# One load of modulation weights split in two, with the scale half in front of the shift half

## The chip, the core and the metric

The kernel runs on one core of a Trainium2 chip. The metric is the device time of one execution in microseconds (us). The core has a matrix engine (TensorE, PE in the profile), whose weight loads are listed apart (PEld), a vector engine (VectorE, DVE), a scalar engine (ScalarE, ACT), GpSimd (POOL) and SyncE (SP), which here does nothing but issue transfers (DMAs). Sixteen DMA engines carry the transfers of all queues.

## The reference

The input is one sequence of 2048 tokens with 640 features in bfloat16. A conditioning vector gives six modulation vectors; the block is an adaptive layer norm ahead of a spectral filter, and another ahead of a gated feed-forward layer.

```
mod = (silu(c) @ w_mod)                 # w_mod: [640, 6*640]
sa, ca, ga, sb, cb, gb = mod split in six
h = layernorm(x) * (1 + ca) + sa
x = x + ga * irfft2(rfft2(h) * W)       # W: [2048, 321] complex
h = layernorm(x) * (1 + cb) + sb
x = x + gb * ((silu(h @ w_gate) * (h @ w_up)) @ w_down)   # 1728 hidden
```

The change concerns sb and cb, the shift and the scale of the second layer norm. Each is the product of a 640-vector with a 640x640 block of w_mod, 800 KB in bfloat16.

## The kernel before

The whole computation is one straight program. The order of the instructions on each engine and in each queue is the order in which the Python code emits them; no scheduler reorders anything. An engine waits in place for the semaphores of what its next instruction needs, and what stands behind it on that engine waits too.

The stages, in order of time:

1. Forward transform (to about 35 us). For each of 16 token tiles TensorE transposes the tile (`t1`), transforms it over the features (`dfwd`) and adds it into a transform over the tokens (`s1`). The result lies in `A_sb`.
2. Spectral filter (to about 63 us). The feature frequencies are worked off in 21 groups of mostly four (`groups`, `NG` = 21). For group g, `stage_a` transforms on TensorE (L567) and multiplies with the filter on VectorE (`prod`, L592); `stage_b` (L599) sums on TensorE; `stage_c` (L620) transforms back; `evac` and `rot` (L637, L648) copy out. The loop runs `stage_a` two groups ahead of `stage_b`.
3. Inverse transform over the token tiles (63 to 82 us), t = 0 to 15: `s1em` and `s1er` (L669, L678) with the table `Htab`, then L1184 and L1187 with the table `RI`, and VectorE adds the residual into `x1` (L1189). `RI` is first multiplied by ga on VectorE (L724, L728). Within this loop the second layer norm of the first two tiles is made: statistics (L761 on ScalarE, L765 to L771), normalization (L775), a transpose by DMA in SP's queue (L789), then scale and shift of the transposed columns, four on GpSimd (L797) and the fifth on ScalarE (L803). TensorE first needs them in `gu13` (L1001).
4. Feed-forward layer in four chunks of 2, 4, 4 and 6 token tiles (82 us to the end): gate and up products (L1013, L1043), down products (L891, L914), residual and store (L883, L884). Some of the weights are combined into tables first; GpSimd issues accumulating loads for that (`gu_dma`, L823).

The modulation weights: `wm_r` holds the four blocks ga, sb, cb, gb of w_mod as `wm_r[:, :, j, :]`, j = 0 to 3, on 128 partitions with 5 rows each. Block 0 is loaded early (L279). Blocks 1 and 2 are loaded by one DMA of 1600 KB (L527), block 3 by one of 800 KB (L528). Both stand in SP's queue behind the four DMA transposes of `A_sb` (`t2_dma`, L519), which wait for the end of stage 1, and ahead of the tables `Htab` and `RI` (L529, L530), the loads of w_down (L734 to L738) and those of the gate and up weights (L741, L742, `load_gu` at L746).

The columns of cb and sb are computed on TensorE in the gaps of the filter stage, as 5 column blocks of 5 matmuls each (`mod_col`, L580), inside `stage_a` behind the group's first matmul. Group NG-4 = 17 takes column blocks 0 and 1 of block j = 2 (scale), group 18 the same of j = 1 (shift), group 19 the rest of the scale, group 20 the rest of the shift:

```
for i, l in enumerate(ls):
    ...
    if i == 0:
        for c5 in {NG - 4: (0, 1), NG - 3: (0, 1), NG - 2: (2, 3, 4), NG - 1: (2, 3, 4)}.get(g, ()):
            mod_col(psum[:, 2 + 2 * (g % 2), 192 + c5:193 + c5], wm_r[:, :, 1 + g % 2], c5)
```

The results are copied at L704 and L705. Block 3 follows behind the last `stage_c` (L719).

Of the kernel before, what the change touches and what calls it, by code (L numbers as in the profile page):

```python
# [155 lines left out]
def adaln_block_kernel(ctx, tc, A_x, A_w_r, A_w_i, B_x, B_w_gate, B_w_up, B_w_down, c, w_mod, out):  # L156
    nc = tc.nc
# [55 lines left out]
    wm_r = rM.cut(12800, [NC5, 4, D])  # L213
# [64 lines left out]
    wm_m = wm_v[:, :, 2 * D:6 * D].rearrange("p k (i d) -> p k i d", i=4)  # L278
# [233 lines left out]
    if True:  # L512
        B2of = {}

        def t2_dma(bi):
            l0 = (1, 16, 32, 64)[bi]
            n = 15 if bi == 0 else 16
            B2b = rL.cut(4096 * bi, [16, 128]) if bi < 3 else rM.cut(6144, [16, 128])
            nc.sync.dma_start_transpose(B2b[:, :n, :], A_sb[:, l0:l0 + n, :, :, :].rearrange("p l t c r -> p l (t c r)"))  # L519
            for i in range(n):  # L520
                B2of[l0 + i] = (B2b, i, l0, n)
# [2 lines left out]
        t2_dma(1)  # L524
        t2_dma(2)
        t2_dma(3)
        nc.sync.dma_start(wm_r[:, :, 1:3, :], wm_m[:, :, 1:3, :])  # L527
        nc.sync.dma_start(wm_r[:, :, 3, :], wm_m[:, :, 3, :])  # L528
        nc.sync.dma_start(Htab[:], H_dram)  # L529
        nc.sync.dma_start(RI[:], RI_dram)  # L530
        Wd_sb = rA.cut(0, [NFC, D])
# [743 lines left out]
@with_exitstack  # L1275
def kernel(
    ctx: ExitStack,
    tc: tile.TileContext,
    A_x: bass.AP,
    A_w_r: bass.AP,  # L1280
    A_w_i: bass.AP,
    B_x: bass.AP,
    B_w_gate: bass.AP,
    B_w_up: bass.AP,
    B_w_down: bass.AP,
    c: bass.AP,
    w_mod: bass.AP,
    out: bass.AP,
):
    with tc.manual_schedule():  # L1290
        adaln_block_kernel(tc, A_x, A_w_r, A_w_i, B_x, B_w_gate, B_w_up, B_w_down, c, w_mod, out)
# [30 lines left out]
```

## Time and profile before

| | |
|---|---|
| time, median of 3 runs | 249.32 us (249.18 to 249.86) |
| the profiled execution's own time | 249.31 us |
| its span, first to last instruction | 247.5 us |
| granted TensorE clock | 1.000 |
| TensorE busy | 241.5 us |
| VectorE / ScalarE / GpSimd busy | 207.7 / 167.8 / 78.1 us |
| the 1600 KB load (L527): issue, time to landing | 48.06 us, 7.32 us |
| the 800 KB load behind it (L528): issue, time to landing | 48.7 us, 10.2 us |

In the profile's lines, L527 is line 527 of the kernel. Times are counted from the start of the span. A timeline's row has start, length, engine, line, operation, output <- input, and the count of instructions merged into the row; in brackets stands the idle time before it and what ended it. Matmuls are pipelined and their ends are modelled, so the starts of successive matmuls say more than the lengths. The names are those of the memory regions: `rM` holds the modulation weights and later `x1`, `rW` the filter and later the gate and up weights, `rA` first `A_sb` and later the w_down weights, `rH` the tables `Htab` and `RI`. In the transfer windows, q1 is the queue that SP issues into and q0 that of GpSimd.

### The profile page before, as it was taken

How to read it: one execution, taken by the hardware profiler on the slowest of the kernel's cores; microseconds unless marked ns; L12 is line 12 of the kernel's file. 1: busy time of each engine (PE TensorE's matmuls, PEld its weight loads, DVE VectorE, ACT ScalarE, POOL GpSimd, SP SyncE). 2: the span in 40 equal slices, each digit the busy share in tenths (PEclk: the TensorE clock that was granted, in tenths of full speed). 3: DMA queues.
4: the chain of work that ended last, by engine and by line, in shares of the span. 5: the costliest groups of instructions: out<-in, count | busy, mean ns of one | idle time of the engine just before them, and what ended most of it. 6: DMA issues, size and time to landing. Idle time of an engine off the chain costs nothing.

```text
span 247.5 us, 6173 instructions
## 1 busy us (share of the span) xinstructions
PE 241.5 (98%) x2327; PEld 189.7 (77%) x2327; DVE 207.7 (84%) x516; ACT 167.8 (68%) x327; POOL 78.1 (32%) x128
## 2 busy tenths in 40 slices
PE   8999999999999999999999999999999999999994
PEld 3778877989999888688887778887765666656773
DVE  3799699988898998789989977788998787789864
ACT  3778757996989698489774488866246777773220
POOL 8577765993243605002004400000432000004400
PEclk9999999999999999999999999999999999999999
DMA  7999999999999999600005110200411000000111
GB/s 220 396 361 315 307 391 177 179 337 392 295 348 317 298 280 187 139 15 3 0 3 106 53 55 3 57 0 19 93 49 53 3 0 1 4 0 0 53 56 53
DMA packets 45760, 34.74 MB, mean 140 GB/s; under 512 B 21732, under 2 KB 42659, under 8 KB 45347
## 3 DMA queue, kind: packets, MB, share of 16 engines
q1 hardware_dynamic: 43936, 30.00, 42.7%
q0 software_dynamic: 1504, 4.28, 7.4%
q8 instruction: 18, 0.29, 0.5%
q10 hardware_dynamic: 290, 0.08, 0.1%
q14 instruction: 12, 0.09, 0.1%
HBM read 27.05 MB, written 4.72 MB: 128 GB/s over the span
## 4 chain that ended last, share of the span: by engine, by line
PE 89%; DVE 4%; DMA 3%; issue 1%; ACT 0%; POOL 0%; DVEq 0%; SPq 0%; ACTq 0%; POOLq 0%
PE psum L1043 36%; PE psum L914 19%; PE psum L1013 6%; PE psum L891 3%; DMA rM<-in_w_mod_dram 3%; PE psum L669 3%; PE psum L599 2%; PE psum L296 2%; PE psum L1184 2%; PE psum L1187 2%; PE psum L1001 2%; PE psum L567 2%; DVE rE L382 2%; PE psum L318 1%; PE psum L315 1%; PE psum L393 1%
## 5 line engine op out<-in xcount | busy, mean ns | idle before, releaser
L1043 PEld LDWEIGHTS <-rW 128*128 128x128 bf16 (+1 forms) x429 | 42.0, 98 | 12.6
L1043 PE MATMUL psum<-rW 128*128 128x256 bf16 (+1 forms) x247 | 42.2, 287 | 0.0
L940 POOL TENSOR_TENSOR rM<-rM,rL 128x320 f32<-128x320 f32 x6 | 5.4, 906 | 96.6 <-ACT rL L939 96.6
L914 PEld LDWEIGHTS <-rE 128*128 128x128 f16 (+1 forms) x196 | 19.0, 97 | 7.8
L914 PE MATMUL psum<-rE 128*128 128x320 f16 (+1 forms) x147 | 22.9, 299 | 0.0
L592 DVE TENSOR_TENSOR rM<-psum,rW 128x384 bf16<-128x384 f32 (+2 forms) x42 | 20.2, 543 | 2.7 <-PE psum L567 1.2
L1074 ACT COPY rH<-psum 128x384 f32<-128x384 f32 (+2 forms) x27 | 14.0, 517 | 7.4 <-PE psum L1043 6.0
L1081 ACT COPY rX<-psum 128x384 f32<-128x384 f32 (+2 forms) x27 | 14.0, 520 | 7.2 <-PE psum L1043 7.0
L1043 PEld LDWEIGHTS <-rE 128*128 128x128 f16 x156 | 15.3, 98 | 4.7
L1078 DVE TENSOR_TENSOR rH<-psum,rM 128x512 bf16<-128x512 f32 (+1 forms) x24 | 15.0, 624 | 4.4 <-PE psum L1043 2.2
L1097 ACT ACTIVATE rL<-psum 128x384 bf16<-128x384 f32 (+2 forms) x27 | 14.4, 533 | 5.3 <-PE psum L1043 3.4
L1082 DVE TENSOR_TENSOR rX<-psum,rX 128x384 f32<-128x384 f32 (+2 forms) x27 | 16.3, 604 | 1.6 <-ACT rX L1081 1.4
L1068 ACT COPY rM<-psum 128x384 f32<-128x384 f32 (+2 forms) x27 | 13.9, 516 | 4.2 <-PE psum L1043 4.2
L382 DVE SCALAR_TENSOR_TENSOR rE<-rE,mv,psum 128x648 bf16<-128x648 f32 (+1 forms) x17 | 14.2, 840 | 2.1 <-PE psum L318 1.7
L1043 PE MATMUL psum<-rW,rE 128*128 128x256 bf16 (+1 forms) x78 | 15.6, 290 | 0.0
L1043 PE MATMUL psum<-rE,rY 128*128 128x256 f16 (+1 forms) x78 | 15.6, 290 | 0.0
L338 ACT COPY rE<-psum 128x640 bf16<-128x640 bf16 x16 | 11.1, 693 | 6.1 <-PE psum L336 5.1
L1098 ACT ACTIVATE rL<-rX 128x384 bf16<-128x384 f32 (+2 forms) x27 | 15.1, 559 | 0.0
L1013 PE MATMUL psum<-rW 128*128 128x256 bf16 x130 | 14.5, 272 | 0.0
L602 ACT CAST rY<-psum 128x512 bf16<-128x512 f32 (+2 forms) x21 | 11.8, 574 | 3.9 <-PE psum L599 3.6
L1189 DVE SCALAR_TENSOR_TENSOR rM<-psum,rX 128x640 f32<-128x640 f32 x16 | 13.0, 820 | 1.7 <-PE psum L1187 1.6
L883 DVE TENSOR_TENSOR rA<-psum,rM 128x320 bf16<-128x320 f32 (+1 forms) x27 | 12.1, 472 | 2.4 <-PE psum L891 2.3
(223 smaller groups left out, 666.5 us busy)
## 6 DMA issues: line engine op xcount, KB each, us to landing
out_dram<-rA SPq DMA_DIRECT2D x31, 80.0 KB, 1.6
rM<-in_w_mod_dram SPq DMA_DIRECT2D x3, 800.0 KB, 10.2
rX<-in_A_x_dram SPq DMA_DIRECT2D x3, 640.0 KB, 7.4
rA<-in_B_w_down_dram SPq DMA_DIRECT2D x2, 960.0 KB, 14.4
rY<-in_B_w_gate_dram POOLq DMA_DIRECT2D x2, 832.0 KB, 7.9
rM<-in_w_mod_dram SPq DMA_DIRECT2D x1, 1600.0 KB, 7.3
rW<-in_B_w_gate_dram SPq DMA_DIRECT2D x2, 640.0 KB, 7.1
rW<-in_B_w_up_dram SPq DMA_DIRECT2D x2, 640.0 KB, 7.1
```

The lines of the kernel that those rows point to most:

```text
L382: nc.vector.scalar_tensor_tensor(Zv[:, h], Cv[:, h], mv[:, t, 0:1], zps[:, h], ALU.mult, ALU.subtract)
L592: nc.vector.tensor_tensor(PP[:, :, hl], xv[:, :, hl], in1, ALU.mult)
L914: nc.tensor.matmul(o, lhsT=lhs[rows(k), k], rhs=rhs[rows(k), k], start=start and k == ks[0], stop=stop and k == ks[-1], skip_group_check=True)
L1013: nc.tensor.matmul(gu[u], lhsT=Wgu[:, u, c5, ff * 128:(ff + 1) * 128], rhs=h2T[:, :, c5, :], start=(c5 == 0), stop=(c5 == NC5 - 1))
L1043: nc.tensor.matmul(o[:, f], lhsT=w, rhs=b, start=(start and f == 0 and i == 0), stop=(stop and f == len(groups[g]) - 1 and i == len(ops) - ...
L1068: nc.scalar.copy(c0, X)
L1074: nc.scalar.copy(c2, X)
L1078: nc.vector.tensor_tensor(c11, Z, c0, ALU.add)
L1081: nc.scalar.copy(c3, X)
L1082: nc.vector.tensor_tensor(c22, Y, c3, ALU.add)
L1097: nc.scalar.activation(g21, X, ACT.Silu, scale=-1.0)
L1098: nc.scalar.activation(g22, c22, ACT.Silu, scale=-1.0)
```

## The change

The one DMA of blocks 1 and 2 becomes two of one block each. The scale block (j = 2) is issued first, then the shift block (j = 1), then block 3 as before, which now is the third turn of the same loop.

```
-        nc.sync.dma_start(wm_r[:, :, 1:3, :], wm_m[:, :, 1:3, :])
-        nc.sync.dma_start(wm_r[:, :, 3, :], wm_m[:, :, 3, :])
+        for j in (2, 1, 3):
+            nc.sync.dma_start(wm_r[:, :, j, :], wm_m[:, :, j, :])
```

The bytes are the same. In w_mod the two blocks lie side by side, so that a row of the one DMA is 2560 contiguous bytes, and a row of each of the two is 1280. SP's queue has one entry more; the order of the others in it, and the order on every other engine, stay. TensorE's wait ahead of the scale columns is now for the scale block alone, and a wait for the shift block stands ahead of the first matmul of the shift columns in group 18. In the kernel after, all three loads carry the line L528, and all other lines keep their numbers.

## The prediction

> **What bounds the kernel now.** I read the page first, then the chain of waits, then timelines and transfer windows around the edited load, and last the first place behind it where another engine joins TensorE.
>
> The page says that TensorE is the bound: 98% of the span, so a gain must come out of its 6 us of gaps.
>
> ```profile
> span 247.5 us, 6173 instructions
> PE 241.5 (98%) x2327; PEld 189.7 (77%) x2327; DVE 207.7 (84%) x516; ACT 167.8 (68%) x327; POOL 78.1 (32%) x128
> ```
>
> The chain of waits between 44 and 68 us (start, length, what) has one transfer in it, the edited one.
>
> ```profile
> 47.88 0.13 SPq L519
> 48.02 0.04 issue
> 48.06 7.32 DMA rM<-in_w_mod_dram
> 55.38 0.05 issue
> 55.43 0.40 PE psum L580 x10
> ```
>
> It leaves SP's queue at 48.06, right behind the last transpose (L519), lands at 55.38, and TensorE starts the scale columns (L580) 0.05 later. How long TensorE stood is in its timeline (start, length, instructions, idle before):
>
> ```profile
> 54.59 0.25 PE L567 MATMUL psum<-Ktab,rM 128*128 128x192 bf16 x1
> 55.43 0.40 PE L580 MATMUL psum<-sc_col,rM 128*128 128x1 bf16 x10 [0.59 <-DMA rM<-in_w_mod_dram]
> ...
> 56.38 0.25 PE L567 MATMUL psum<-Ktab,rM 128*128 128x192 bf16 x1
> 56.46 0.39 PE L580 MATMUL psum<-sc_col,rM 128*128 128x1 bf16 x10
> ```
>
> The second pair, which waited for nothing, starts 0.08 us apart; the first pair 0.84 apart. The stall is worth 0.76 us of issue time (the 0.59 counts from the modelled end of the matmul). The line at 56.46 is the first use of the shift columns, 1.03 us behind the scale columns, and no wait stands before it: both halves are in one transfer today.
>
> **The change, part by part.** The sum is made against the profiled execution's 249.31 us (span 247.5 and 1.8 around it), 0.01 below the median of 249.32.
>
> *Removed:* the wait for 1600 KB before the scale columns. The 800 KB of the scale go first. Transfers start slowly here (42 packets of 2560 B between 48.9 and 50.4 us), then run at full rate:
>
> ```profile
> DMA packets 157, 0.40 MB, mean 402 GB/s; under 512 B 0, under 2 KB 0, under 8 KB 157
> ```
>
> That is 52.5 to 53.5 us. From 50.4 on, 0.82 MB take 2.0 us at this rate; with the tail of the slowest engine (about 1 us: the load would be through at 54.4 by rate and landed at 55.38) the scale lands by 53.5, over 1 us before TensorE can use it at 54.59 + 0.08 = 54.67. **Gain there: 0.76 us**, and PE's place at the shift columns moves to 56.46 - 0.76 = 55.70.
>
> *Added:* a second wait, PE's for the shift half. The same bytes have passed by then, in rows of 1280 B in place of 2560. The neighbour L528, of just this shape, moves between 55 and 56 us as follows:
>
> ```profile
> DMA packets 289, 0.37 MB, mean 370 GB/s; under 512 B 0, under 2 KB 289, under 8 KB 289
> ```
>
> One engine is busy with something else in that window, so 370 against 402 GB/s is the dear bound: 1.64 MB take 0.35 us longer. The cheap bound is 0: from 52 to 54 us (2560 B alone) 403 GB/s flowed, from 54 to 56 (nearly all 1280 B) 388. I take 0.2. The shift half then lands at 55.38 + 0.2 = 55.58, 0.12 ahead of its use; at the dear bound it comes at 55.73 and costs 0.1. **Term: 0.** Behind that wait stand the rest of the group's transforms and all of TensorE, and DVE's products (L592), which wait for them.
>
> *SP's queue:* one more issue of about 0.52 us (L528's row) ahead of the last gate columns, Htab, RI and the W_down loads. Nothing is fetched later for that: the transfer engines are full from 50.4 on and those wait behind bytes, not behind the issue. What they do inherit is the 0.2. Their covers, after PE's move: column 3 at 58.9 + 0.2 for a use at 62.18 - 0.76; Htab at 61.46 + 0.2 for 63.03 - 0.76 = 62.27; RI at 62.23 + 0.2 for DVE's L724 at 63.32 - 0.76 = 62.56. RI is the tightest, 0.13; beyond that it costs one to one, up to 0.15 at the dear bound. **Term: 0.**
>
> [...]
>
> *Given back further on.* From 55.4 to 80 us TensorE has hardly a gap, DVE and ACT wait for it, and all move 0.76 forward. The next thing that does not hang on TensorE is the transposed, normalized input of the first token chunk: SP's L789 issues the transpose at 72.19, it lands at 78.09, GpSimd scales four of five columns (L797), TensorE uses them at 80.79.
>
> ```profile
> 70.20 0.84 POOL L823 DMA_DIRECT2D rY<-in_B_w_gate_dram  x1
> 78.22 2.50 POOL L797 TENSOR_SCALAR rW<-rW,one_p_cb,modcols 128x256 bf16<-128x256 bf16 x4 [7.17 <-DMA rW<-rL]
> ```
>
> ```profile
> 80.79 0.71 PE L1001 MATMUL psum<-rW,Wp 128*128 128x256 bf16 x5
> ```
>
> L1001's matmuls stand 0.11 apart, so the fourth, which needs GpSimd's last column (80.72, plus 0.05), runs at 81.11. **The slack is 0.34 us, less than the 0.76 that TensorE brings**; what decides is whether the landing at 78.09 moves too. It is a matter of bytes: the third gate/up load (L746, issued 68.35) and GpSimd's 832 KB load (L823) are ahead of the transpose. Between 74.5 and 75 us L823's queue has the engines for itself:
>
> ```profile
> DMA packets 60, 0.20 MB, mean 399 GB/s; under 512 B 0, under 2 KB 0, under 8 KB 60
> ## 3 DMA queue, kind: packets, MB, share of 16 engines
> q0 software_dynamic: 60, 0.20, 114.0%
> ```
>
> L823 follows GpSimd's chain from DVE's first L1189 and so also starts 0.76 earlier, into the third L746 load. At 73.0 - 0.76 = 72.24 that load has 0.2 MB (200 packets after 73.0) + 0.76 us x 0.354 MB/us + the inherited 0.07 = 0.54 MB left; with L823's 0.85 MB that is 1.39 MB at 0.39 MB/us, 3.6 us, ending at 75.8. The same sum for today's order gives 75.7 where the trace ends at 76.3, so I allow 75.8 to 76.3 and take 76.1 for the transpose's first packet (today 75.1). Its data need 1.3 us (492 packets in the half microsecond from 77.0, some 1280 in all) if its list is ready, 2.3 as today (75.1 to 77.4) if it starts slowly, and 0.65 to land. That is 78.05 to 79.05; I take 78.25, near the quick end, as it will have been queued for a microsecond. GpSimd is then through 78.25 - 78.09 = 0.16 later than today, TensorE's L1001 comes 0.34 - 0.16 = 0.18 earlier, and behind it TensorE runs without a gap to the end.
>
> **Sum:** -0.76 at L580, +0.58 at L1001: -0.18, **249.1 us**. Its own range: landing 77.9 to 78.5, 248.8 to 249.4.
>
> **The rivals.**
>
> *All of it is kept* (0.20): the transpose lands 0.42 earlier or more, because it has its list early and slips in between the two loads. An unloaded transpose of this size (L789 at 155.60) takes 3.8 us, from 71.43 that is 75.2. Against it: one queue, in order, with the third L746 load ahead. 249.31 - 0.76 = 248.55.
>
> *Slower, at the same join* (0.16): the transpose starts at 76.3, has today's slow 2.3 us and lands at 79.25. GpSimd ends 1.16 later, TensorE loses 1.16 - 0.34 = 0.82: 250.1. The deciding point is a landing after 78.43; 79.2 makes 0.3%. For it: the transpose's packets were slow even with the engines half idle.
>
> *Slower, at the shift half* (0.04): the second half does not flow behind the first but starts anew, in the 2.3 us from issue (48.06) to full rate (50.4). It lands at 57.7, against 56.46 today: +1.2, 250.5. Against it: between 54 and 55 us packets of both sizes flow without a pause. [...]
>
> *It does not do what it says* (0.12): the scale half does not land before the whole does, or a late engine holds the shift half to 56.4 (an instruction fetch of 16 KB occupied one engine for 1.06 us from 54.89 on). Nothing is won: 249.3.
>
> **How the numbers follow.** The forecast has 0.48. A measurement of this kernel can tell about 0.3%, 0.75 us. Faster by more: only the first rival, whose 248.55 is just past the line of 248.57, three quarters of it and a little for the sum's errors, 0.17. Slower by more: the two slower ones, 0.20, rounded up to 0.21. Within: the rest, 0.62. The range from 248.5 to 250.2 takes in the whole gain, the forecast and the slower join, and leaves out some 0.15: the 250.5 and both tails.
>
> **What would show it.** Right: no wait at the scale columns, L580 near 54.67; a landing of the shift half near 55.6; L1189 and L669 0.7 earlier; L823 issued near 69.5 and the transpose landing near 78.2; a wait of GpSimd's column now ahead of L1001's fourth matmul. Wrong: a wait for the shift half of over 0.3, Htab or RI as releasers, or a transpose that lands before 77.7 or after 78.6.

## The result and the profile after

The changed kernel takes 251.05 us (median of 22 runs, 249.27 to 252.98); the kernel before, run beside it, 249.96 us (22 runs, 249.00 to 251.73). The ratio is 1.0055, with a 95% interval from 1.0035 to 1.0075. Ratios leave out runs over 1.5% above the kernel's fastest: here none, further on two of the changed kernel and one of the fill. The forecast was 249.1, the range 248.5 to 250.2: **slower, where a small gain was expected, and outside the range.**

The profile after shows nothing of that loss. Its execution took 249.27 us, the shortest of the 22, and the page reads almost as before:

```profile
span 247.5 us, 6176 instructions
PE 241.4 (98%) x2327; PEld 189.5 (77%) x2327; DVE 207.9 (84%) x516; ACT 167.9 (68%) x327; POOL 78.0 (32%) x128
```

Same span, same busy times. So the first lesson comes ahead of any cause: this one profile is of an execution in which the cost did not occur, and typical ones are shown further on. In TensorE's timeline after (start, length, instructions) the edit does what it was to do:

```profile
55.36 0.25 PE L567 MATMUL psum<-Ktab,rM 128*128 128x192 bf16 x1
55.44 0.39 PE L580 MATMUL psum<-sc_col,rM 128*128 128x1 bf16 x10
...
56.39 0.25 PE L567 MATMUL psum<-Ktab,rM 128*128 128x192 bf16 x1
56.47 0.39 PE L580 MATMUL psum<-sc_col,rM 128*128 128x1 bf16 x10
```

Scale columns and shift columns both start 0.08 us behind the matmul ahead of them: neither half is waited for. Yet the scale columns stand at 55.44, where they stood at 55.43 before. TensorE itself arrived 0.77 later (L567 at 55.36, against 54.59). The reason lies 16 us earlier, in VectorE's timeline after, with the idle time and its releaser in brackets:

```profile
39.43 0.43 DVE L407 TENSOR_TENSOR rW<-rW 128x512 bf16<-128x512 bf16 x1 [0.75 <-DMA rW<-wflip_r]
```

And the same instruction in the profile of before:

```profile
38.66 0.42 DVE L407 TENSOR_TENSOR rW<-rW 128x512 bf16<-128x512 bf16 x1
```

A load of filter weights landed later, VectorE stood 0.75 for it, and the whole filter stage was put back by 0.77. It is over 8 us ahead of the first edited instruction, and it varies among profiles of the kernel before too (L407 from 38.66 to 39.05 in four of them, and L567 ahead of the scale columns stands 15.9 behind it in each). Further on, GpSimd's scaling starts 0.23 later than before and TensorE does not wait for it:

```profile
78.45 2.43 POOL L797 TENSOR_SCALAR rW<-rW,one_p_cb,modcols 128x256 bf16<-128x256 bf16 x4 [7.40 <-DMA rW<-rL]
```

```profile
80.80 0.70 PE L1001 MATMUL psum<-rW,Wp 128*128 128x256 bf16 x5
```

### The profile page after: what moved, and what is told of

It reads as the page before. It is cut to its first block, busy times and chain, and to the rows that moved or that the text cites. A ratio compares the mean times of both kernels' runs of the same rounds, so it can differ in the third digit from the quotient of the medians.

```text
span 247.5 us, 6176 instructions
## 1 busy us (share of the span) xinstructions
PE 241.4 (98%) x2327; PEld 189.5 (77%) x2327; DVE 207.9 (84%) x516; ACT 167.9 (68%) x327; POOL 78.0 (32%) x128
## 4 chain that ended last, share of the span: by engine, by line
PE 81%; SPq 10%; DMA 6%; DVE 1%; issue 1%; ACT 0%; DVEq 0%; ACTq 0%
PE psum L1043 36%; PE psum L914 19%; PE psum L1013 6%; DMA rW<-wflip_r 4%; PE psum L599 3%; PE psum L891 3%; PE psum L669 3%; SPq L273 2%; PE psum L567 2%; SPq L277 2%; SPq L275 2%; PE psum L620 2%; PE psum L1184 2%; DMA rM<-in_w_mod_dram 2%; PE psum L1187 2%; PE psum L1001 2%
```

## The experiments

### Both kernels again, and two ways to part the edit

Three theories stood against each other at this point, by the names that the expectations use. Clock: without the pause TensorE's clock is lowered in some executions (8 of the 22 runs of after have a mean of 0.992 or 0.993). Transfer: the split or its additional queue entry makes transfers land later further on, as in the rival *slower, at the same join*, where L1001 waits for L797 and L797 for the transpose's landing. Chance: the two kernels differ by nothing that lasts. Four kernels on one chip: before unchanged, after unchanged, after with the shift half in front (TensorE then needs both halves at its first column, as before), and before with the load of block 3 cut in two instead (the wait as before, one more entry).

```
# shift first
-        for j in (2, 1, 3):
+        for j in (1, 2, 3):
# one more entry
-        nc.sync.dma_start(wm_r[:, :, 3, :], wm_m[:, :, 3, :])
+        nc.sync.dma_start(wm_r[:, 0:3, 3, :], wm_m[:, 0:3, 3, :])
+        nc.sync.dma_start(wm_r[:, 3:5, 3, :], wm_m[:, 3:5, 3, :])
```

Before unchanged:

> The kernel of before, unchanged, to see its spread and the granted clock of each of its runs beside those of the kernel after. In 22 runs the kernel after had eight at a granted clock of 0.992 to 0.993 (251.5 to 253.0 us), three at 0.998 (250.3 to 250.6) and eleven at 1.000 (249.3 to 252.1, median 250.8). Clock theory (the extra time is TensorE held back where the pause before the scale columns no longer rests it): nearly all runs of this kernel stand at 1.000, median 249.3 to 250. Transfer theory (the split makes transfers land later further on, and the clock is chance): low clocks are as frequent here as in the kernel after, and at 1.000 this kernel is about 0.8 us faster than the kernel after. Chance theory (the two differ by nothing that lasts): the same spread for both, medians within 0.3 us.

After unchanged:

> The kernel after, unchanged, on the same chip as the kernel before. Clock theory: a third to a half of its runs below 0.995, and those alone make it slower than before; runs at 1.000 equal to or up to 0.8 us faster than before's. Transfer theory: slower by about 0.8 us in runs at 1.000 too, and the trace has a new wait for a transfer between 55 and 100 us. Chance theory: within 0.3 us of before.

Shift first:

> The same split with the halves in the order shift, scale, block 3: the scale half lands where the whole landed before, so TensorE's pause of 0.76 us stays, and everything else of the split (1280-byte rows, one more transfer in the queue) is kept. Clock theory: as before, 249.3 to 250.0, clocks of 1.000. Transfer theory: as the kernel after or slower, +0.8 to +1.6 us. Chance theory: as before within 0.3 us.

One more entry:

> The 1600 KB load stays whole; in its place block 3 is cut in two transfers (480 and 320 KB), so that the queue has one entry more and every later transfer moves one place in the ring of semaphores, as in the kernel after, but the scale columns wait as before and rows stay 2560 bytes. Clock theory: as before. Transfer theory, if it is the additional queue entry: as the kernel after, +0.8 us; if it is the 1280-byte rows: as before. Chance theory: as before within 0.3 us.

Measured, beside a common 249.84 us: before 250.16, ratio 1.0016 [0.9986, 1.0046]; after 250.95, **1.0044 [1.0016, 1.0073]**; shift first 250.05, **1.0008 [0.9983, 1.0033]**; one more entry 249.47, 0.9997 [0.9972, 1.0023]. So the loss is repeatable, and by the medians neither the split of the transfer nor the added entry is enough for it: it goes when TensorE again waits for both halves, though the intervals of after and of shift first overlap. The transfer theory had put shift first 0.8 us or more above the kernel before, which missed; the clock theory had put it where it came, and is tested further on. In the timeline of shift first TensorE waits for both halves for 1.0 us (the starts are 1.11 apart, 0.08 without a wait):

```profile
55.15 0.25 PE L567 MATMUL psum<-Ktab,rM 128*128 128x192 bf16 x1
56.26 0.40 PE L580 MATMUL psum<-sc_col,rM 128*128 128x1 bf16 x10 [0.86 <-DMA rM<-in_w_mod_dram]
```

**Removing the pause gains nothing here: the kernels that have it are not the slower ones.** What the pause does is seen 25 us later, at the join.

### Two typical profiles of the changed kernel

> The kernel after, unchanged, one look for another trace: its traces so far (248.9 and 249.3 us) are of the fastest of its 34 runs, so neither shows where a typical run (250.8 to 250.9) loses its time. Join theory (TensorE comes earlier to stage 3, the chunk's transposed input does not, GpSimd's load collides with it): in a run of over 250 us TensorE stands at the first L1001 or behind it for 0.5 to 2 us. Clock theory: such a run has the same order of waits and a stretch with a granted clock under 1. Upstream theory (a late filter load, which the pause used to absorb): TensorE is late by over 0.8 us already at L580.

> The kernel after again, for one more trace. Join theory: a run over 250 us stands at the first L1001; clock theory: it has a stretch under a granted clock of 1; upstream theory: it is late at L580 already.

They took 251.16 and 250.74 us, as most runs of after do. In both the join stalls. GpSimd's timeline and TensorE's in the first of them:

```profile
80.68 2.43 POOL L797 TENSOR_SCALAR rW<-rW,one_p_cb,modcols 128x256 bf16<-128x256 bf16 x4 [9.61 <-DMA rW<-rL]
```

```profile
81.28 0.27 PE L1001 MATMUL psum<-rW,Wp 128*128 128x256 bf16 x1 [0.39 <-POOL rW L797]
82.08 0.27 PE L1001 MATMUL psum<-rW,Wp 128*128 128x256 bf16 x1 [0.53 <-POOL rW L797]
82.63 0.27 PE L1001 MATMUL psum<-rW,Wp 128*128 128x256 bf16 x1 [0.27 <-POOL rW L797]
83.17 0.38 PE L1001 MATMUL psum<-rW,Wp 128*128 128x256 bf16 x2 [0.27 <-POOL rW L797]
```

From the first to the last start these five take 0.43 us when nothing is late, and 1.99 here (81.28 to 83.27, the second of the last row standing 0.11 behind the first): 1.56 lost. The first one also starts 0.69 behind the row ahead of it (L1187 at 80.59) and not 0.23 as in the profile after (80.57 to 80.80): 0.46 more, **2.0 us in all**. The second profile lost 1.64 and 0.37, again 2.0. The chain of waits of the first names the transpose:

```profile
72.22 8.28 DMA rW<-rL
80.50 0.02 issue
...
80.68 2.44 POOL rW L797 x4
83.12 0.04 issue
83.17 0.38 PE psum L1001 x2
```

The same transfer took 5.9 us in the profiles of before and of after above. Its packets (256 bytes) show two parts of this. They begin late, at 76.03 and 75.78, against 74.45 to 75.18 in four profiles of before. And the last come at 79.38 and 78.98: a fetch of 16 KB of TensorE's instructions, of 1.11 us (78.13 on, and 77.83), got in ahead of the transpose's last 6 and 3 packets. (The fetches are queue q8 of the page: in the profile of before 18 packets and 0.29 MB, one to some 259 of TensorE's 4654 matmuls and weight loads. That they are TensorE's is read from this and from the two runs further on in which a fetch comes earlier once matmuls are added ahead of it.) All other packets were through at 78.36 and 78.02, 2.3 and 2.2 us behind the first, as in the profile of before (75.18 to 77.51). An estimate from these rows: with the usual 0.6 from the last packet to the landing (77.51 to 78.09 before) and 0.15 more to GpSimd's start, L797 would have started at 79.1 and 78.8 in place of 80.68 and 80.17. So about 1.5 of the 2.0 us are the fetch, and about 0.5 the late begin. The transfer window from 78.7 to 79.3 us of the first profile:

```profile
DMA packets 2, 0.00 MB, mean 1 GB/s; under 512 B 2, under 2 KB 2, under 8 KB 2
```

Next to nothing but the fetch, begun before the window (78.13 to 79.24), is under way; then the transpose's remainder comes in. In the first profiles of before and after the fetch starts too (77.44, 77.58), but in the last 0.1 us of the transpose, with no packet behind it.

### Hold TensorE's place, or mend the join

Two repairs of the changed kernel tell the place of TensorE from the join. In one, matmuls on a constant fill TensorE for 0.75 us ahead of the scale columns. In the other GpSimd issues its 832 KB load (L823) only when tile 5's residual is done, which puts those bytes behind the transpose.

```
# fill: in stage_a, ahead of mod_col
+                    if g == NG - 4:
+                        idle_pe(3)
+                        idle_pe(1, 2)
# hold: ahead of the first gu_dma
             if t in (8, 11):
+                if t == 8:
+                    nc.gpsimd.tensor_copy(warm[:], st2[:, 5, 0:1])
                 gu_dma(...)
```

> The kernel after, with 0.75 us of additional matmuls of ones on TensorE (three of 512 columns, one of 256, results overwritten) ahead of the scale columns, where the kernel before pauses. TensorE is as late at all that follows as in the kernel before, but it is not at rest. Clock theory (it is the rest that counts): as the kernel after or worse, a third of the runs at 0.991 to 0.993, median 250.5 to 251.5. Join theory (it is the earlier arrival that counts): as the kernel before, 249.5 to 250.2, clocks nearly all above 0.996.

> The kernel after, with GpSimd's first 832 KB load (L823) held back until the statistics of tile 5 are there, some 2 us later, so that it comes behind the transposed input of the first chunk in the transfer engines and not ahead of it. Join theory: that input lands 1 us or more earlier, L1001 does not wait, the gain of 0.76 us is kept: 249.0 to 249.3, faster than the kernel after by over 1 us. Clock theory: nothing changes against the kernel after, median 250.5 to 251.5 with the same low clocks. Upstream theory: as the kernel after.

Fill: 250.75 us, 1.0031 [0.9999, 1.0062], no cure, where the join theory had expected 249.5 to 250.2. Part of the time may be the fill's own 0.75 us, since TensorE has hardly a gap. But the join stalls in its profile as well: TensorE reached the scale columns and L1001 where it did in the first profile of before (55.42 and 80.77, against 55.43 and 80.79), the fetch cut off 13 packets, and L1001 lost 1.5 us. So TensorE's place alone does not decide. A fixed delay moves TensorE back but does not tie it to the queue, as a wait would; that this is the reason is argued, not shown. Hold: **249.61 us, 0.9979 [0.9951, 1.0008]**, and the loss is gone. By the clock theory it should have stayed, for TensorE rests no more here than in after. The same hold was then put into the kernel before and run beside the held after:

> The kernel before (one 1600 KB load, TensorE's pause kept) with GpSimd's first 832 KB load held back behind the chunk's transpose. Join theory: the landing of the transpose moves 1.5 us or more ahead of need, so late landings no longer stop TensorE; the spread shrinks and the median falls a little against before, 249.2 to 249.6. What the split is then worth is read against the kernel after with the same hold: 0.4 to 0.76 us by the first term of the prediction. Clock theory (rest of TensorE at the scale columns): no difference from before, and slower by nothing.

> The kernel after with the same hold, again, on the same chip as the one above. If the pause of 0.76 us is really gone and nothing else takes it: 0.4 to 0.76 us faster than the kernel before with the hold. If the split has a price of its own in the transfer queue: equal or slower.

Before with hold 249.74 us, **0.9973 [0.9952, 0.9993]**; after with hold 249.86, 0.9983 [0.9961, 1.0004]. GpSimd's timeline of the former:

```profile
73.48 0.18 POOL L1198 COPY warm<-st 128x1 f32<-128x1 f32 x1 [2.79 <-DVE rM L1189]
74.03 0.83 POOL L823 DMA_DIRECT2D rY<-in_B_w_gate_dram  x1 [0.36 <-ACT rL L673]
76.49 2.41 POOL L797 TENSOR_SCALAR rW<-rW,one_p_cb,modcols 128x256 bf16<-128x256 bf16 x4 [1.62 <-DMA rW<-rL]
```

L823 leaves at 74.0 instead of 70.2, L797 starts at 76.5, and L1001 (81.24) finds its columns 2 us ahead. Three things follow. The join is the place of the loss. It costs the kernel before something too, for the hold makes that faster. And with the join out of the way the split brings nothing that can be measured: the two held kernels are 0.1% apart, with the split on the slower side. A gain of 0.36 us, the mean pause of the four profiles of before, would be 0.14% and inside these intervals; the 0.76 of the prediction, 0.30%, would hardly be.

### A later transpose, and an earlier fetch

> The kernel after with the chunk's transpose (L789) issued behind one more 640 KB load (the up half of L746) in place of ahead of it, so that it always lands late, by some 1.7 us of transfer. Join theory: TensorE stands at the first L1001 for 2 to 4 us in every run, and the median rises by at least 1.5 us over the kernel after, to 252.5 or more. Clock as a consequence of the stand: most runs have a granted clock of 0.992 to 0.993, that is one window of about 3.4 us at half clock behind the stand, and cost up to 1.7 us more. Clock theory in its first form (the missing rest at the scale columns lowers the clock): low clocks as frequent as in the kernel after, a third.

Here the transpose (L789) was issued behind one more 640 KB load, the rest as in after.

```
             if t == 4:
+                load_gu(512, 1024, (1,))
                 ln2_tr(0)
-                load_gu(512, 1024, (1,))
                 load_gu(1024, 1664)
```

253.15 us (4 runs), 1.0108 [1.0064, 1.0152]. The join scales with the landing: L797 started at 81.50, and TensorE lost 2.7 us. And a second cost shows itself. Three of the four runs had a mean clock of 0.992 or 0.993. By stretches of 2 us of the profiled one (busy time and instructions of PE, PEld, DVE, ACT and POOL; then the granted clock, the transfer share and GB/s):

```profile
82.00:84.00 2.00, 1.08 (x6) 0.54 (x6) 1.00 (x5) 0.00 (x0) 2.00 (x5) 1.00 1.07 364
84.00:86.00 2.00, 2.00 (x13) 1.54 (x12) 0.98 (x3) 0.38 (x1) 2.00 (x3) 0.54 1.00 235
86.00:88.00 2.00, 2.00 (x13) 1.47 (x11) 1.02 (x3) 1.11 (x4) 1.23 (x2) 0.61 0.82 145
88.00:90.00 2.00, 2.00 (x21) 1.78 (x19) 1.97 (x7) 2.00 (x4) 0.00 (x0) 1.00 1.08 211
```

TensorE's clock is halved from 84.16 to 87.58, 3.41 us, right behind the stand at L1001: 13 matmuls in 2 us in place of 21. Half of 3.41 is 1.7 us, and 1.7 of 251.6 is the 0.7% that the mean clock, 0.993 here, lacks. Ahead of it TensorE stood only in pieces, 1.33 us and three of 0.27 to 0.28, 2.1 us in all. In the two stalled profiles of after the pieces came to some 1.5 us (0.27 to 0.58 each), and the clock stayed at 1.000. What makes the clock fall, and why only some runs have the low clock, no run here shows.

The changed kernel has such a clock (0.991 to 0.993) in 10 of its 34 timed runs, the kernel before in 2 of 110, the held kernels in none of 36. Of the 1.09 us between the two medians of the result, the 14 runs of after at 0.997 and above leave 0.67 (median 250.63); the rest, some 0.4, goes with the runs of low clock, which can also be those with the longest stand. That the low clock sits behind L1001 in those runs as well is inferred from this one trace; no execution of after with a low clock was profiled.

The fetch was tested from two sides. In the kernel before, 12 matmuls of one column in the pause put TensorE's program 24 instructions ahead (each has its weight load):

```
                 if i == 0:
+                    if g == NG - 4:
+                        for _ in range(12):
+                            nc.tensor.matmul(banks(5, 1, [1]), lhsT=ones[:], rhs=ones[:, 0:1], start=True, stop=True)
```

> The kernel before with 12 additional one-column matmuls (24 instructions, some 0.3 us) inside TensorE's pause before the scale columns, so that nothing gets later but TensorE's instruction stream is 24 instructions further at every later point, and each block of 256 instructions is fetched some 0.8 us earlier against the transfers. Fetch theory (a 16 KB instruction fetch gets in front of the last packets of the chunk's transpose on one transfer engine): late landings as in the kernel after, median 250.5 to 251.2 and some runs at 0.992. Without it (the landing is late only by queue and by TensorE's place): as before, 249.6 to 250.1.

250.76 us, **1.0031 [1.0004, 1.0058]**: the kernel before gets slower by these matmuls, although its profile still has a pause (0.23 from the start of the last one to the scale columns). Part of that can be their own time: they start from 55.08 to 55.36, some 0.3 us, and an execution without a pause pays it. The transfer window from 77.5 to 78.5 us shows the other part:

```profile
DMA packets 17, 0.01 MB, mean 5 GB/s; under 512 B 16, under 2 KB 17, under 8 KB 17
q1 hardware_dynamic: 17, 0.01, 12.4%
```

The fetch began at 77.01, 19 packets of the transpose stood behind it, and these 16 are nearly all that moves in a microsecond. L797 started at 79.53 and L1001 lost 0.48. TensorE itself is not held up in the fetch: its first matmuls of L669 for successive tiles (L672 in this kernel) start at 75.87, 76.98, 78.09 and 79.19, 1.10 to 1.11 apart. The transfer behind the fetch is.

The other side is the changed kernel with the fetch moved away, by replacing four of the warm-up matmuls of the first 5 us (512 columns take 0.45 us each there in the profile of before, and 0.22 from 6.78 us on) with 64 short ones:

> The kernel after with part of the matmuls that keep TensorE warm during its first 5 us (four of 512 columns) replaced by 64 of one column, so that its instruction stream is 120 instructions further everywhere and the fetch that fell at 77.3 to 78.5 us, at the end of the chunk's transpose, falls about 4 us earlier, the next one 4.7 us later. The order of transfers and the work stay. Fetch theory: no packets of the transpose behind a fetch, large late landings vanish: median 249.6 to 250.2, no run at 0.991 to 0.993, faster than the kernel after by 0.7 us or more. Queue theory (the transpose is late because the queue is, the fetch is a bystander): as the kernel after, 250.7 to 251.1 with a fifth to a third of the runs below 0.994.

> The kernel before, one look. Upstream reading (the 0.76 us of the first trace were a large draw, as TensorE was early there): TensorE stands before the scale columns for 0 to 0.4 us. If 0.76 is usual: 0.6 to 0.9. At the first L1001 a small loss or none (first to fifth matmul 0.4 to 1.6 us apart), no packets of the transpose behind the fetch.

> The kernel before, one more look. The same expectations: a stand of 0 to 0.4 us before the scale columns, no packets of the transpose behind the fetch at 77 to 78 us.

> The kernel after, one more look. No stand before the scale columns; with a chance of one half packets of the transpose behind the fetch, and then 1.5 us or more lost at the first L1001 and a time over 250.5 us.

The fetch did move, to 73.22, but the edit also made TensorE reach the scale columns 1.4 us late (56.82), the transpose still took from 75.85 to 79.46, and the time was 251.13, 1.0081 [1.0054, 1.0107]. The fetch theory had expected 249.6 to 250.2, which missed; but the late TensorE can account for 1.4 us by itself, and L1001 lost only 0.3 (its five starts from 82.16 to 82.94, against 0.43 undisturbed). So the run settles little. This transpose was slow without TensorE's fetch inside it, and what slowed it is open. Three more profiles, of 249.18 and 248.91 (before) and 249.49 us (after), serve the following table.

### All profiles side by side

| profile | us | pause before L580 | transpose's first packet behind L580's start | data packets behind the fetch | L1001 lost |
|---|---|---|---|---|---|
| before, four | 249.31 | 0.76 | 19.75 | 0 | 0 |
| | 249.72 | 0.08 | 20.10 | 0 | 1.14 |
| | 249.18 | 0.58 | 19.12 | 0 | 0 |
| | 248.91 | 0 | 19.61 | 0 | 0 |
| after, five | 249.27 | 0 | 19.95 | 0 | 0 |
| | 248.92 | 0 | 19.90 | 0 | 0 |
| | 251.16 | 0 | 20.57 | 6 | 2.0 |
| | 250.74 | 0 | 20.72 | 3 | 2.0 |
| | 249.49 | 0 | 20.03 | 0 | 0.18 |
| shift first | 250.07 | 1.03 | 19.93 | 0 | 0 |
| one more entry | 250.48 | 0 | 19.71 | 0 | 1.2 |

The fourth column is where the change should show: how far the transpose comes behind TensorE's own place. Its mean is 19.65 in before and 20.23 in after, 0.6 more, though the single values overlap (19.12 to 20.10, and 19.90 to 20.72). Two terms would make that up. The split load holds the queue some 0.3 us longer (from its first packet to the 2.45th MB 7.42 to 7.59 in the table's six profiles with the split, 7.13 to 7.31 in the five others), and the mean pause of 0.36 is gone. Shift first has the late queue (76.19) but a TensorE held back by the same queue, and loses nothing. The stalls are in the rows above 20.0, but for one more entry. There, and in the second row, the last data packet was early enough (77.83 and 77.07) and the landing came 2.0 us behind it, not 0.6. Each transpose ends with 32 packets of 4 bytes (77.39 to 77.53 in the profile of before); in these two profiles the last of them came only when the fetch ended (78.78 and 78.02). So each row that lost 1 us or more has a packet of the transpose behind the fetch, and no other row has. Apart from those packets the data took 2.1 to 2.6 us in all eleven.

How often the stall occurs is read from the times. The profiled executions overlap (249.72 with 1.14 lost, 250.07 without a loss), and the runs are from several chips, so the count is rough. I put the line at 250.3 when the times were known, between the two groups of after. Above it are 29 of 34 runs of after, 45 of 132 of before, 5 of 12 of shift first, 4 of 12 of one more entry, 8 of 12 of fill, 9 of 12 with the earlier fetch, and 4 of 36 with the hold.

## Why the prediction was wrong, point by point

- **"Gain there: 0.76 us": mis-sized.** The scale half is never waited for, as forecast. But 0.76 was the pause of one execution, the largest of four profiles of before (0.76, 0.08, 0.58, 0; mean 0.36). It depends, among other things, on when the filter load lands for L407. I read a variable wait from one profile as a constant.
- **Shift half, term 0: right.** Its wait was 0 in all profiles of after and 0.16 in one of the held ones.
- **The split's cost in the queue, 0.2: nearly right,** some 0.3.
- **Htab and RI, term 0: right.** The chain of waits after has no transfer in it from 44 to 68 us.
- **Landing "78.05 to 79.05; I take 78.25": the step that decided, wrong.** The first packet was forecast for 76.1; in the two stalled profiles it came at 76.03 and 75.78. But the packets took 3.2 to 3.35 us, and not 1.3 to 2.3, and the landing came at about 80.0 and 80.5, past the 78.6 that the prediction names as a sign of being wrong. In the two fastest profiles of after GpSimd started at 78.45 and 78.31, so there the transpose landed as forecast. The price that was missing is the instruction fetch ahead of the last packets, about 1.5 us by the estimate above. I had seen a fetch at 54.89, 1.06 us long, and used it for another rival only, not for the small transfer with a tight slack.
- **"The slack is 0.34 us" and the deciding point of 78.43: right.** With TensorE at L1001 at 80.8 a start of L797 at 78.45 lost nothing; with TensorE 0.2 later a start at 78.97, half a microsecond later, lost 0.18. Among the unheld profiles of the two kernels all the later starts stalled.
- **The rival *slower, at the same join*, 0.16 and 250.1: the right mechanism, with too little chance and too small a price.** 0.82 was the loss forecast; 2.0 was measured twice, and the halved clock adds 1.7 in the one run of low clock that was profiled (the later transpose). I gave the forecast 0.48 because I took the landing near its quick end, while TensorE's lead and the queue's delay both worked against the same 0.34.
- **The rival *slower, at the shift half*: did not come true.** The shift half was waited for in none of the five profiles of after; by this rival it was to cost 1.2 us.
- **What the edit removed.** I counted the pause as waste. When the queue is late the pause makes TensorE late too, and so it can meet the join 25 us later. The profile of shift first shows that once (transpose at 76.19, pause of 1.03, no loss); that it is why the kernel before loses less often is argued from the medians, and the shares of the queue's delay and of TensorE's lead are not parted. When a fetch is asked for, and why it is served ahead of the last packets in some executions, is open.

## What to carry to other kernels

Before a wait is taken away, look for the next place where the engine meets the same queue, and compare its slack with the time gained plus what the queue loses; if the slack is smaller, mend that join first. Here the join was worth 0.27% by itself (a load held until a small transpose is through), and the wait nothing that could be measured. And take a wait's size from several profiles: the runs of this kernel before spread over 1% (249.00 to 251.73 in the result), its pause was anything from 0 to 0.76, and the first profile was of the largest.

## What the runs showed of the hardware that I had not expected

- An instruction fetch of 16 KB at the join took 1.0 to 1.1 us in the nine profiles of the two kernels. A transpose with 6 of its 1280 packets behind it landed 2 us later than one with none (80.5 against 78.3).
- Around such a fetch the transfers nearly stood in two profiles, for 1.3 and 1.2 us (78.7 to 80.0, and 77.5 to 78.7: 2 to 12 GB/s), with loads of 800 KB issued and not complete; in the other stalled profile of after (250.74 us) the loads flowed on. What holds the queue is not known.
- A stand of TensorE in pieces, of 2.1 us in all, was followed by one stretch of 3.41 us at half clock, 1.7 us of work; after 1.5 us in pieces, in two profiles, none followed.
- The landing of one and the same filter load, ahead of anything edited, moved TensorE's place by over 1 us among profiles (L567 ahead of the scale columns from 54.59 to 55.81, 15.9 behind the L407 that waits for the load in every profile but that of the fetch moved away).
